# Retention and a gated feed-forward on one core: y's factors on GpSimd, four VectorE operations per weight tile, loads held by landings, a new order in the first third

## The chip and the metric

One core of a Trainium2 chip. The metric is the time of one execution on the device in microseconds (us). The engines are named as in the profile: PE is TensorE's matmul, PEld its weight load, DVE is VectorE, ACT is ScalarE, POOL is GpSimd, SP is SyncE, which here issues every DMA.

## What is computed

Inputs q, k, v have shape 4 x 8 x 768 x 64 (batch, head, time, width). In float32:

```python
for t in range(S):
    state = gamma[None, :, None, None] * state + np.einsum('bhd,bhe->bhde', k[:, :, t], v[:, :, t])
    y[:, :, t] = scale * np.einsum('bhd,bhde->bhe', q[:, :, t], state)
...
h = np.maximum(x @ w_in, 0.0)
...
for k in range(K):
    conv_out += conv_w[k][None, None, :] * hp[:, k:k + S, :]
gate = 1.0 / (1.0 + np.exp(-conv_out))
return (h * gate @ w_out).astype(np.float32)
```

gamma depends on the head alone, x is y with its heads side by side (4 x 768 x 512), hp is h with a row of zeros at both ends of time, K is 3, w_in is 512 x 1024 and w_out 1024 x 512. The weights arrive as 64-bit floats, and the kernel makes 32-bit floats of them itself, from their two 32-bit words.

## The kernel before

**Retention.** A chunk is 64 steps of time of two batches and eight heads; there are 24, twelve for each pair of batches. `scores` (L396 through `multiply`) multiplies k and q, `masked` (L423) multiplies the scores by a triangular mask, `scale_v` (L364 on ACT, L367 on DVE) scales v by powers of gamma, `mix` sends the masked scores times v and, from chunk 3 on, the next chunk's scores to PE in alternation, and `across` sends q times the carried state and the update of the state. `carry` (L430) copies the state out of PSUM, `decay` (L437) multiplies y by a factor for the chunk, `gy`. The factors of a pair's eleven later chunks are one first factor `gy_0`, loaded, times one number per chunk and head; `make_gy` (L354) makes them for four chunks at a time on DVE. `x_head` (L447, ACT) and `x_rest` (L453, DVE) split y into a coarse part and its rest, which PE takes in the format that the profile calls fp32r.

**Weights.** There are 16 tiles of 128 x 512, tiles 0 to 7 of w_in and 8 to 15 of w_out, and one 128 x 24 tile (number 16) of the convolution's weights. A tile is loaded (`load_w`, L463, 512 KB) and then made float32: `w_abs` on ACT (L481, absolute value of the high word), then on DVE `w_clamp` (L486), `w_shift` (L491), `w_sign` (L499), `w_power` (L507), `w_low` (L515, the low word times a power of two). `w_head` (L532, ACT) is the coarse part, `w_rest` (L547) the rest, and `w_add` (L562) adds the low word to the rest. Seven operations of a tile are on DVE.

**Feed-forward.** A unit is two chunks (twelve units). `mm1` (L576) multiplies a unit by one tile of w_in, 12 matmuls of 256 columns; from unit 6 on, units are taken in pairs by `prod` (L696) with sums of weight blocks made by `sum_w`, `w_head_t` and `w_rest_t`. `relu`, `conv_tap`, `conv_side`, `gate`, `gated`, `g_head`, `g_rest` follow on ACT and DVE, `seam` copies border columns on POOL (L744, L746), `mm2` (L793) multiplies by w_out, six matmuls of 512 columns a call, `put` and `store` write out.

**What sets the order.** Each engine takes its instructions in the order of the list `ORDER`, written out by hand; buffers are chosen by the strings in `SLOTS` and the addresses in `PLACES`. All loads and stores go through SP's queue in the order of the list, so one that waits holds the later ones. A load waits for its buffer; `HELD` adds a wait for a computing step to seven of them. Chunks 0 to 3 (`ALONE`) are loaded in two halves, `load` (q and k, L335) and `load_kv` (k and v, L339), 512 KB each; later chunks in one load of 1024 KB. There are three buffers `rw` for chunks. At the start PE runs `FILL` products of no use (L318), and `WARM` names a step ahead of which three shorter ones (L312) stand.

Of the kernel before, what the change touches and what calls it, by code (L numbers as in the profile page):

```python
# [59 lines left out]

WARM = {
    "mix/0": 3,
# [26 lines left out]
    scale_v/5 w_rest/4 w_clamp/16 w_low/4 relu/1/0 mm1/1/3 w_shift/16 load/7 scale_v/6 w_sign/16 w_add/4 w_power/16
    w_low/5 mix/5 relu/1/1 decay/4 w_abs/6 w_rest/5 across/5 w_clamp/6 w_low/16 w_add/5 mm1/1/4 carry/5 load/8  # L90
    decay/5 load_w/8 x_head/4 masked/6 w_abs/7 mm1/0/4 w_shift/6 w_add/16 w_sign/6 w_power/6 w_head/6 mix/6
    make_gy/2 conv_tap/0/2 across/6 w_clamp/7 scale_v/7 w_shift/7 masked/7 mm1/0/5 load/9 load_w/9 w_sign/7 carry/6
    conv_tap/0/3 w_low/6 mm1/1/5 relu/0/2 w_rest/6 w_head/7 seam/0/2/0 w_power/7 seam/0/1/0 w_add/6 mix/7 w_rest/7
    w_abs/8 across/7 w_low/7 x_head/5 relu/1/2 w_add/7 mm1/0/6 load/10 x_rest/4 w_clamp/8 x_rest/5 mm1/0/7 w_shift/8
    scale_v/9 w_sign/8 mm1/2/0 relu/0/3 masked/8 w_abs/9 scale_v/8 carry/7 mm1/2/1 w_power/8 w_head/8 load_w/10
    w_clamp/9 conv_tap/0/0 load_w/11 decay/7 mm1/1/6 w_shift/9 w_low/8 w_sign/9 mix/8 decay/6 w_head/9 scale_v/10
    across/8 masked/9 seam/0/0/0 seam/0/2/2 seam/1/2/0 mix/9 x_head/6 x_head/7 carry/8 w_power/9 relu/2/0
    conv_tap/0/1 conv_side/0/0/0 w_rest/8 w_add/8 load/11 seam/2/0/0 conv_tap/0/4 seam/5/0/2 seam/0/1/2 seam/0/0/2
    decay/8 masked/10 conv_side/0/4/0 w_low/9 seam/1/0/2 conv_side/0/1/0 x_rest/6 conv_side/0/1/2 mm1/1/7 relu/1/3
    mm1/2/2 mm1/2/3 mm1/2/4 mm1/2/5 w_abs/10 w_clamp/10 w_shift/10 w_abs/11 conv_side/0/0/2 gate/0/0 w_clamp/11  # L100
    gated/0/0 w_shift/11 across/9 carry/9 w_rest/9 w_sign/10 w_power/10 x_head/8 relu/2/1 x_rest/7 relu/2/2 x_rest/8
    mix/10 across/10 carry/10 decay/9 conv_side/0/3/2 w_sign/11 conv_side/0/2/0 x_head/9 mm1/3/2 mm1/3/3 relu/3/1
    mm1/3/4 mm1/3/5 g_head/0/0 w_add/9 w_power/11 w_low/11 conv_side/0/2/2 g_rest/0/0 mm2/0/1/0/0 masked/11 x_rest/9
    conv_tap/0/5 conv_side/0/5/2 conv_side/0/4/2 w_low/10 decay/10 conv_side/0/5/0 relu/3/2 seam/2/2/2 seam/1/0/0
    scale_v/11 load/12 w_head/11 w_rest/11 w_add/11 mm2/0/0/0/0 mix/11 masked/12 across/11 decay/11 load/13
    conv_tap/0/6 scale_v/12 w_head/10 conv_side/0/3/0 gate/0/1 w_rest/10 gated/0/1 across/12 load_w/14 w_abs/14
    w_clamp/14 mix/12 decay/12 masked/13 conv_tap/0/7 seam/2/2/0 seam/1/1/0 seam/4/2/0 carry/12 load_w/13 w_abs/13
    w_clamp/13 w_shift/13 mm1/2/6 mm1/2/7 relu/2/3 load/14 mm1/3/0 mm1/3/1 w_shift/14 w_sign/14 g_head/0/1 mm1/4/4
    mm1/4/5 w_add/10 g_rest/0/1 mm2/0/0/1/0 w_power/14 w_sign/13 w_head/13 mm2/0/1/1/0 seam/0/3/2 relu/3/0
    scale_v/13 mix/13 across/13 conv_side/0/7/2 seam/1/2/2 seam/1/3/0 seam/2/1/2 seam/2/1/0 w_power/13 w_low/13  # L110
    conv_tap/1/0 conv_side/1/0/2 w_head/14 seam/3/3/0 conv_side/0/6/2 conv_side/1/0/0 w_rest/13 scale_v/14 w_add/13
    seam/0/3/0 seam/3/1/0 conv_side/0/7/0 gate/0/2 x_head/10 gated/0/2 seam/4/0/0 seam/1/1/2 seam/2/0/2 seam/2/3/0
    conv_side/0/6/0 load_w/12 conv_tap/1/1 conv_side/1/1/0 conv_side/1/1/2 gate/0/3 x_head/11 gated/0/3 masked/14
    g_head/0/2 g_rest/0/2 gate/1/0 relu/4/2 w_abs/12 gated/1/0 w_clamp/12 x_rest/11 conv_tap/1/4 conv_tap/1/5
    conv_side/1/5/2 conv_side/1/4/2 load_w/15 w_abs/15 w_clamp/15 w_shift/12 w_shift/15 w_low/14 w_sign/15
    w_power/15 w_rest/14 mm1/3/6 mm1/3/7 relu/3/3 mm1/4/0 mm1/4/1 w_head/15 w_sign/12 carry/13 w_head/12 relu/4/0
    w_add/14 w_power/12 w_low/12 w_rest/12 conv_side/1/4/0 seam/1/3/2 mm1/4/2 mm1/4/3 relu/4/1 load/15 x_rest/10
    mix/14 across/14 mm1/4/6 mm1/4/7 g_head/1/0 carry/14 g_rest/1/0 mm1/5/2 mm1/5/3 w_low/15 conv_side/1/5/0
    conv_tap/1/6 gate/1/2 w_add/12 decay/14 diff/0/0/3 gated/1/2 seam/3/1/2 g_head/0/3 g_rest/0/3 conv_tap/1/2
    mm2/0/1/2/0 w_rest/15 w_add/15 conv_side/1/2/2 g_head/1/2 conv_tap/1/7 conv_side/1/6/0 masked/15 conv_tap/1/3  # L120
    scale_v/15 sum_w/0/7 conv_side/1/7/0 conv_side/1/6/2 relu/5/1 mm2/0/0/2/0 mm2/0/1/3/0 mm2/0/0/3/0
    conv_side/1/3/0 conv_side/1/7/2 conv_side/1/2/0 conv_side/1/3/2 gate/1/1 put/0/1/0 g_rest/1/2 gated/1/1
    g_head/1/1 load/16 mix/15 seam/6/3/0 seam/3/0/0 gate/1/3 across/15 carry/15 conv_tap/2/4 conv_tap/2/5 mm1/5/4
    mm1/5/5 seam/2/3/2 scale_v/16 diff/0/0/1 seam/3/2/0 mm2/1/0/0/0 g_rest/1/1 mm2/1/0/1/0 mm2/1/0/2/0 gated/1/3
    conv_side/2/4/2 sum_w/0/0 conv_tap/2/0 conv_side/2/0/2 g_head/1/3 g_rest/1/3 conv_tap/2/2 put/0/0/0 mm2/1/1/0/0
    mm2/1/1/1/0 diff/0/0/2 conv_side/2/5/2 sum_w/0/8 sum_w/0/9 conv_side/2/5/0 decay/15 conv_side/2/4/0 masked/16
    gate/2/2 conv_tap/2/1 head/0/0/0 decay/13 diff/0/1/3 conv_side/2/0/0 gated/2/2 g_head/2/2 diff/0/1/1
    conv_side/2/1/2 conv_side/2/1/0 conv_side/2/2/0 load/17 scale_v/17 g_rest/2/2 conv_tap/2/6 conv_tap/2/7
# [743 lines left out]
```

## Time and profile before

| what | us |
|---|---|
| median of 3 runs (lowest, highest) | 334.76 (332.27, 334.77) |
| span of the profiled execution | 331.0 |
| PE busy in it | 322.2 |
| DVE busy | 288.7 |
| ACT busy | 215.0 |
| POOL busy | 26.1 |

The page gives the profiled execution's span, from its first to its last instruction; its time as a run is not listed apart, and what lies around the span is read from the median of the runs. An engine counts as busy while it works on an instruction of its own; fill products count too. In the lists of the trace an engine's idle time stands in brackets before the instruction that ended it, with the engine or transfer that released it.

### The profile page before, as it was taken

The numbers are of one execution on the slowest core, as the hardware profiler recorded it, in microseconds if no ns is written. First come the engines' busy times: TensorE is split into PE (matmuls) and PEld (weight loads), VectorE is DVE, ScalarE is ACT, GpSimd is POOL, SyncE is SP. The second block draws the span as 40 slices with busy tenths as digits, with TensorE's granted clock in tenths as the row PEclk, the third lists the DMA queues.
The fourth block names the chain that finished last, engine by engine and source line by source line (L and its number), as shares of the span: only waits on it lengthen the run. The fifth ranks groups of instructions, "written<-read, shape, count | busy, mean of one in ns | idle before, by whom it ended". The sixth has DMA issues, their size and how long they took to land.

```text
span 331.0 us, 10761 instructions
## 1 busy us (share of the span) xinstructions
PE 322.2 (97%) x4642; PEld 289.4 (87%) x4642; DVE 288.7 (87%) x566; ACT 215.0 (65%) x448; POOL 26.1 (8%) x100
## 2 busy tenths in 40 slices
PE   8888999999999999899999999999999999999996
PEld 3778999999999988798888989999999888987885
DVE  3999999999999999897999998779988887869980
ACT  4657774756666475755939664965796866776761
...
GB/s 256 386 331 338 251 311 266 197 159 239 180 168 153 130 100 63 160 264 139 51 192 34 34 0 35 34 2 7 25 34 0 64 1 64 3 63 0 65 63 63
DMA packets 10415, 40.77 MB, mean 123 GB/s; under 512 B 1280, under 2 KB 1792, under 8 KB 7808
## 3 DMA queue, kind: packets, MB, share of 16 engines
...
q8 instruction: 36, 0.59, 0.7%
q14 instruction: 11, 0.09, 0.1%
...
## 4 chain that ended last, share of the span: by engine, by line
PE 94%; DMA 4%; issue 0%; ACT 0%; DVE 0%; ACTq 0%
PE ps_o L793 40%; PE ps_m L576 20%; PE ps_m L696 8%; PE ps_y L696 8%; PE ps_s L396 5%; PE ps_st L396 4%; DMA rw<-in_qkv 4%; PE ps_y L396 4%; PE ps_s L696 3%; PE ps_o L318 2%; PE ps_o L312 0%; ACT rw L364 0%; ACT o_sb L800 0%; DVE o_sb L304 0%; ACTq L800 0%
## 5 line engine op out<-in xcount | busy, mean ns | idle before, releaser
L576 PE MATMUL ps_m<-xu,wi_hi 128*128 128x256 f32 x384 | 68.8, 283 | 0.0
L793 PE MATMUL ps_o<-h,g 128*128 128x512 f32 (+1 forms) x200 | 62.7, 382 | 0.0
L576 PEld LDWEIGHTS ps_m<-xu,wi_hi 128*128 128x128 f32 x384 | 58.4, 189 | 0.9
L576 PE MATMUL ps_m<-xu,wi_lo 128*128 128x256 f32 x192 | 53.5, 279 | 0.0
L764 ACT ACTIVATE cv<-cv 128x512 f32<-128x512 f32 x48 | 29.8, 630 | 34.0 <-DVE cv L758 34.0
L396 PE MATMUL ps_y<-rw 64*64 64x64 f32 x1472 | 48.4, 220 | 0.1
L396 PEld LDWEIGHTS ps_y<-rw 64*64 64x64 f32 x1472 | 45.2, 135 | 0.7 <-ACT rw L629 0.4
L793 PEld LDWEIGHTS ps_o<-h,g 128*128 128x128 f32 x200 | 37.2, 188 | 7.1 <-ACT o_sb L800 0.4
L779 DVE TENSOR_TENSOR g<-cv,g 128x512 fp32r<-128x512 f32 x48 | 32.6, 687 | 8.1 <-ACT g L774 7.4
L758 DVE SCALAR_TENSOR_TENSOR cv<-h,cw_sb,cv 128x256 f32<-128x256 f32 x84 | 38.7, 478 | 1.0 <-ACT cv L753 0.4
L774 ACT CAST g<-cv 128x512 fp32r<-128x512 f32 x48 | 29.3, 617 | 11.7 <-DVE cv L769 10.3
L576 PEld LDWEIGHTS ps_m<-xu,wi_lo 128*128 128x128 f32 x192 | 36.1, 188 | 0.0
L396 PEld LDWEIGHTS ps_s<-rw 64*64 64x64 f32 x768 | 24.4, 135 | 8.6 <-issue 3.2
L396 PE MATMUL ps_s<-rw 64*64 64x64 f32 x768 | 27.6, 221 | 4.0 <-DMA rw<-in_qkv 1.5
L396 PE MATMUL ps_st<-rw 64*64 64x64 f32 x704 | 25.0, 219 | 0.5 <-ACT rw L364 0.5
L364 ACT ACTIVATE rw<-rw,consts_sb 128x128 f32<-128x128 f32 x64 | 20.4, 391 | 6.4 <-DMA rw<-in_qkv 6.4
L396 PEld LDWEIGHTS ps_st<-rw 64*64 64x64 f32 x704 | 22.6, 135 | 1.5 <-ACT rw L364 1.0
L753 ACT ACTIVATE cv<-h,cw_sb 128x256 f32<-128x256 f32 x42 | 20.5, 504 | 2.0 <-DVE g L779 2.0
L800 ACT COPY o_sb<-ps_o 128x512 f32<-128x512 f32 (+1 forms) x25 | 13.9, 561 | 11.8 <-PE ps_o L793 11.7
L423 DVE TENSOR_TENSOR rw<-ps_s,consts_sb 128x512 f32<-128x512 f32 x24 | 16.4, 684 | 5.2 <-PE ps_s L396 5.2
L793 PE MATMUL ps_o<-h_m,g 128*128 128x512 f32 (+1 forms) x50 | 19.1, 384 | 0.0
L793 PE MATMUL ps_o<-h_s,g 128*128 128x512 f32 (+1 forms) x50 | 19.1, 384 | 0.0
(256 smaller groups left out, 758.4 us busy)
## 6 DMA issues: line engine op xcount, KB each, us to landing
...
```

What stands on the lines that cost most here:

```text
L364: nc.scalar.activation(v[:, :, g], v[:, :, g], AF.Copy, scale=by[:, g : g + 1])
L396: nc.tensor.matmul(out, lhsT, rhs, start=start, stop=stop, skip_group_check=True)
L423: nc.vector.tensor_tensor(out=rw[n][:, 1], in0=s_ps[n], in1=mask_sb.unsqueeze(1).broadcast_to([P, 2, NPAIR, C]), op=ALU.mult)
L576: nc.tensor.matmul(h_ps[u, p][:, odd], w[:, k, fs], x[:, k].rearrange("p b t -> p (b t)"), start=(i == 0), stop=(i == len(products) - 1),)
L696: nc.tensor.matmul(ps[:, i], w[k][:, fs], x[:, k].rearrange("p b t -> p (b t)"), start=(i == m == 0 and q in (1, 5)), stop=(m == len(produ ...
L753: nc.scalar.activation(cvs[u, p][:, i], hs[u, p][:, i, :, 1 : P + 1], AF.Copy, scale=cw_sb[:, f, 1:2])
L758: nc.vector.scalar_tensor_tensor(out=cv, in0=h[:, :, k : k + P], scalar=cw_sb[:, f, k : k + 1], in1=cv, op0=ALU.mult, op1=ALU.add)
L764: nc.scalar.activation(cvs[u, p], cvs[u, p], AF.Sigmoid)
L774: nc.scalar.copy(gs[u, p][:, 0], cvs[u, p])
L779: nc.vector.tensor_tensor(out=lo, in0=cvs[u, p], in1=hi.bitcast(F32), op=ALU.subtract)
L793: nc.tensor.matmul(ps, g, w[f][:, cs], start=(f == 0 and i == 0), stop=(f == NF - 1 and i == 2))
L800: nc.scalar.copy(o[:, :n], o_ps[u, t, h][:, :n])
```

## The change

- `make_gy` makes one chunk's factor at a time, on POOL instead of DVE, into two buffers in turn; it stands 22 times in the list.
- A weight tile: `w_abs` scales the value down while taking it; `w_low3`, new and on ACT, turns the low word into the three bits that are still wanted; `w_clamp` has one comparison; `w_join`, new on DVE, shifts and puts the three bits in; `w_sign` puts the sign in; `w_rest` writes the rest in place. `w_shift`, `w_power`, `w_low` and `w_add` are gone.
- Each load waits until an earlier load has landed: the nearest one with at least eight units (`AHEAD`) issued after it, where a half chunk or a weight tile counts four units, a whole chunk eight, the constants three and `gy_0` one. `HELD` is gone.
- The buffers that the sums of weights take among the three `rw` are taken when the first of them is written.
- `FILL` is 5 instead of 6, the three warm products stand before mix/2 instead of mix/0, and the list has a new order up to about the products of unit 6.

```diff
-GY_AT_ONCE = 4
+AHEAD = 8
+SIZES = {"load_consts": 3, "load_gy": 1, "load_kv": 4, "load_w": 4, "load": 4}
...
-FILL = 6
+FILL = 5
...
-    load_w/0 load_w/1 load/0 load_consts load_kv/0 load_w/2 load/1 load_kv/1 load_gy load/2 w_abs/0 w_clamp/0
-    w_shift/0 w_sign/0 w_abs/1 w_power/0 w_head/0 w_clamp/1 w_rest/0 scores/0 w_low/0 masked/0 scale_v/0 w_add/0
-    w_shift/1 w_abs/2 mix/0 w_sign/1 w_clamp/2 w_shift/2 carry/0 load_kv/2 scores/1 w_power/1 load/3 w_head/1
-    load_w/3 masked/1 load_w/16 scale_v/1 w_low/1 w_sign/2 mix/1 decay/0 across/1 make_gy/0 carry/1 w_head/2
-    w_rest/1 load_kv/3 scores/2 load/4 decay/1 scale_v/2 masked/2 x_head/0 w_add/1 scores/3 x_head/1 w_power/2
-    w_abs/3 x_rest/0 mix/2 x_rest/1 load_w/4 w_clamp/3 across/2 scale_v/3 w_shift/3 masked/3 mm1/0/0 load/5 w_low/2
-    load_w/5 w_rest/2 mm1/0/1 w_sign/3 decay/2 w_head/3 w_add/2 carry/2 mix/3 w_abs/16 w_power/3 w_abs/4 w_rest/3
...
+    load_w/1 w_abs/1 w_low3/1 w_clamp/1 w_join/1 w_sign/1 load/0 load_consts load_kv/0 scale_v/0 scores/0 load_kv/1
+    load/1 masked/0 mix/0 scores/1 masked/1 scale_v/1 load_w/2 w_abs/2 carry/0 mix/1 across/1 w_low3/2 load_w/3
+    w_abs/3 w_clamp/2 load/2 load_kv/2 w_join/2 w_clamp/3 w_sign/2 w_low3/3 load_gy w_join/3 load_w/0 load/3
+    scores/2 masked/2 w_sign/3 w_head/2 carry/1 make_gy/1 scale_v/2 w_head/1 decay/0 mix/2 decay/1 across/2 scores/3
+    w_head/3 load_kv/3 x_head/0 w_low3/0 x_rest/0 w_rest/2 load_w/16 x_head/1 x_rest/1 make_gy/2 seam/0/0/0
+    make_gy/3 load/4 w_abs/0 carry/2 mm1/0/2 scale_v/3 decay/2 w_rest/3 mm1/0/3 w_clamp/0 w_join/0 x_head/2
+    w_low3/16 masked/3 mix/3 w_sign/0 w_head/0 w_rest/0 w_rest/1 w_abs/16 across/3 scale_v/4 decay/3 x_rest/2
+    load_w/6 load_w/4 mm1/0/0 relu/0/1 mm1/0/1 x_head/3 w_low3/4 load_w/5 make_gy/5 x_rest/3 w_abs/4 relu/0/0
...
     def make_gy(n):
+        gys[n] = const.tile([P, NPAIR, C], F32, name="gy_sb", bufs=2)
+        nc.gpsimd.tensor_tensor(
+            out=gys[n], in0=gy_0, in1=gf[:, n % NC].unsqueeze(2).broadcast_to([P, NPAIR, C]), op=ALU.mult
         )
...
-        nc.scalar.activation(m, high.bitcast(F32), AF.Abs)
+        nc.scalar.activation(m, high.bitcast(F32), AF.Abs, scale=EXP_DOWN)
+    def w_low3(i):
+        low = pieces[i][0].bitcast(U32)
+        nc.scalar.activation(low, low, AF.Copy, scale=LOW_BITS)
...
-        nc.vector.tensor_scalar(out=m, in0=m, scalar1=EXP_LOW, scalar2=EXP_HIGH, op0=ALU.max, op1=ALU.min)
+        nc.vector.tensor_scalar(out=m, in0=m, scalar1=EXP_HIGH, scalar2=None, op0=ALU.min)
+    def w_join(i):
+        low, _, m = pieces[i]
+        mi = m.bitcast(I32)
+        nc.vector.scalar_tensor_tensor(
+            out=mi, in0=mi, scalar=3, in1=low, op0=ALU.logical_shift_left, op1=ALU.bitwise_or
         )
...
+    def behind():
+        between = 0
+        for load, size in reversed(loads):
+            if between >= AHEAD:
+                return load
+            between += size
```

The order of the retention steps and products on PE up to chunk 23 is, in the part that the prediction speaks of, before: `mix/17 across/17 mix/18 across/18 mm1/5/6 mm1/5/0`; after: `mix/17 across/17 mm1/4/3 mm2/1/1/0/0 mm2/1/0/1/0 mm2/1/1/1/0 mix/18 across/18`. Both have `mix/11 across/11 across/12 mix/12` with nothing between.

## Rows read from the trace of the kernel before

**Rows 1.** The page: shares of the span, the instruction queue, the chain by engine.
```profile
PE 322.2 (97%) x4642; PEld 289.4 (87%) x4642; DVE 288.7 (87%) x566; ACT 215.0 (65%) x448; POOL 26.1 (8%) x100
...
q8 instruction: 36, 0.59, 0.7%
...
PE 94%; DMA 4%; issue 0%; ACT 0%; DVE 0%; ACTq 0%
```

**Rows 2.** Waits of PE: us in total, times, longest.
```profile
PE ps_s L396 <- issue: 1.3, 1, 1.3
```

**Rows 3.** Stretches: PE, PEld, DVE, ACT, POOL busy (instructions), clock, DMA share, GB/s.
```profile
0.00:30.00 30.00, 25.57 (x572) 20.05 (x573) 23.13 (x42) 17.43 (x40) 0.38 (x7) 1.00 0.93 329
10.00:15.00 5.00, 4.08 (x149) 3.31 (x150) 4.35 (x9) 3.86 (x10) 0.00 (x0) 1.00 1.07 400
30.00:130.00 100.00, 100.00 (x2039) 94.36 (x2037) 97.96 (x194) 62.04 (x132) 9.78 (x30) 1.00 0.55 193
130.00:200.00 70.00, 68.71 (x1257) 60.52 (x1256) 65.46 (x128) 47.34 (x101) 3.93 (x17) 1.00 0.30 104
200.00:331.00 131.00, 127.95 (x781) 114.51 (x779) 102.12 (x205) 88.16 (x176) 12.01 (x46) 1.00 0.09 33
```

**Rows 4.** The chain in order of time: start us, us, what.
```profile
1.05 6.92 PE ps_o L318 x12
9.05 1.49 PE ps_o L312 x6
11.73 5.07 DMA rw<-in_qkv
17.35 8.26 DMA rw<-in_qkv
27.95 3.02 PE ps_m L576 x24
138.93 1.29 issue
204.25 1.36 PE ps_o L793 x6
```

**Rows 5.** Timelines of PE, ACT, DVE at the start: start us, us, what [idle before].
```profile
12.08 1.15 PE L396 MATMUL ps_s<-rw 64*64 64x64 f32 x32 [0.44 <-DMA rw<-in_qkv]
18.74 1.09 PE L396 MATMUL ps_s<-rw 64*64 64x64 f32 x30 [1.29 <-DVE rw L423]
21.63 0.50 PE L576 MATMUL ps_m<-xu,wi_hi 128*128 128x256 f32 x2
25.75 0.33 PE L396 MATMUL ps_s<-rw 64*64 64x64 f32 x4 [1.03 <-DMA rw<-in_qkv]
...
16.82 1.28 ACT L364 ACTIVATE rw<-rw,consts_sb 128x128 f32<-128x128 f32 x4 [0.28 <-DMA rw<-in_qkv]
...
19.54 1.28 DVE L453 TENSOR_TENSOR xu<-x,xu 128x512 fp32r<-128x512 f32 x2
```

**Rows 6.** Groups by line of DVE and ACT: busy us, mean ns, idle before.
```profile
L515 DVE SCALAR_TENSOR_TENSOR g<-g 128x512 f32<-128x512 uint32 x16 | 11.0, 686 | 0.1
L507 DVE TENSOR_SCALAR g<-m 128x512 int32<-128x512 int32 x16 | 6.7, 423 | 0.1
L562 DVE TENSOR_TENSOR wi_lo<-m,g 128x512 fp32r<-128x512 f32 x8 | 5.5, 685 | 0.1
L354 DVE TENSOR_TENSOR gy_sb<-consts_sb 128x1024 f32<-128x1024 f32 (+1 forms) x3 | 3.4, 1128 | 0.0
...
L481 ACT ACTIVATE m<-g 128x512 f32<-128x512 f32 x16 | 10.8, 684 | 5.0 <-DMA g<-in_w_in 4.6 <-DVE wi_lo L562 0.4
```

**Rows 7.** Groups by line of POOL: busy us, mean ns, idle before.
```profile
L744 POOL COPY h<-h 128x4 f32<-128x4 f32 x16 | 6.0, 387 | 116.7 <-ACT h L588 58.7 <-ACT h L585 52.7 <-DVE cv L769 5.3
...
L744 POOL COPY h_o<-h 128x4 f32<-128x4 f32 x1 | 1.2, 1170 | 1.2 <-ACT h L585 1.2
```

**Rows 8.** All weight loads (L463), issue to landing.
```profile
DMA to landing us min/median/max: 3.3/5.8/8.5
```

More of the change, by code (lines that the diff above doesn't have):

```diff
@@ L89 @@
[L89 to L128, printed above, removed]
@@ new lines @@
+    w_clamp/4 make_gy/4 w_join/4 w_clamp/16 mm1/1/0 mm1/1/1 mm1/1/2 mm1/1/3 w_sign/4 w_head/4 masked/4 w_abs/5
+    w_low3/5 w_clamp/5 w_join/5 w_sign/5 w_rest/4 w_low3/6 w_abs/6 carry/3 load/5 w_clamp/6 w_head/5 w_rest/5
+    w_join/6 w_join/16 mix/4 across/4 load/6 load_w/7 masked/5 w_sign/16 relu/1/0 scale_v/5 mm1/0/4 mm1/0/5 w_low3/7
+    carry/4 relu/1/1 mix/5 across/5 load_w/8 load_w/10 w_sign/6 decay/4 w_head/6 load/7 w_rest/6 relu/0/2 w_low3/8
+    w_abs/7 x_head/4 mm1/1/6 mm1/1/4 w_clamp/7 w_join/7 decay/5 w_sign/7 w_abs/8 w_clamp/8 masked/6 w_low3/10
@@ new lines @@
+    scale_v/6 carry/5 mm1/1/5 x_head/5 scale_v/7 relu/1/2 mix/6 w_head/7 across/6 carry/6 w_rest/7 mm1/0/6 mm1/0/7
+    load/8 load_w/12 w_low3/12 w_abs/12 x_rest/5 masked/7 mix/7 across/7 x_rest/4 w_clamp/12 load_w/9 conv_tap/0/0
+    conv_tap/0/2 w_low3/9 w_abs/9 w_join/8 w_sign/8 w_head/8 relu/0/3 mm1/1/7 mm1/2/0 mm1/2/1 w_clamp/9 w_join/9
+    relu/1/3 conv_tap/0/1 carry/7 mm1/2/6 conv_side/0/0/0 make_gy/6 seam/0/1/0 decay/6 x_head/6 conv_tap/0/3
+    w_sign/9 w_head/9 load/9 scale_v/8 masked/8 w_rest/8 make_gy/9 make_gy/7 w_abs/10 w_clamp/10 decay/7 seam/0/0/2
@@ new lines @@
+    conv_tap/0/6 mix/8 w_join/10 scale_v/9 w_sign/10 w_rest/9 seam/2/0/0 seam/1/0/0 make_gy/8 seam/0/3/0 seam/0/1/2
+    relu/2/0 seam/1/0/2 across/8 mm1/2/7 mm1/2/2 carry/8 load_w/14 seam/0/2/2 seam/2/1/0 masked/9 decay/8 w_join/12
+    conv_side/0/1/0 conv_side/0/1/2 load_w/13 load/10 conv_side/0/2/2 conv_side/0/0/2 conv_tap/0/7 x_rest/6 relu/2/3
+    w_abs/14 gate/0/0 x_head/7 w_clamp/14 mix/9 across/9 carry/9 masked/10 scale_v/10 conv_side/0/3/0 gated/0/0
+    mm1/2/3 conv_side/0/3/2 mm1/2/4 w_sign/12 load/11 w_low3/14 w_join/14 w_sign/14 mix/10 across/10 g_head/0/0
@@ new lines @@
+    x_head/8 x_rest/8 x_rest/7 g_rest/0/0 w_head/10 mm1/2/5 w_rest/10 decay/9 masked/11 conv_side/0/6/0
+    conv_side/0/7/0 conv_side/0/2/0 relu/2/2 mm2/0/1/0/0 load/13 load_w/11 load/12 w_head/12 make_gy/11 seam/0/3/2
+    conv_side/0/7/2 conv_side/0/6/2 make_gy/10 seam/3/0/0 relu/2/1 seam/2/2/0 load_w/15 w_low3/11 mm1/3/2 w_low3/13
+    mm1/3/4 mm1/3/5 mm1/3/3 x_head/9 scale_v/11 carry/10 scale_v/12 w_head/14 w_abs/11 decay/10 x_rest/9
+    conv_tap/1/0 gate/0/1 mix/11 across/11 across/12 w_clamp/11 masked/12 w_join/11 gated/0/1 conv_tap/1/1 relu/3/2
@@ new lines @@
+    w_sign/11 w_rest/12 mix/12 sum_w/0/0 carry/12 gate/0/3 w_rest/14 decay/12 masked/13 relu/3/1 w_head/11 mm1/3/0
+    mm1/3/1 mm1/3/6 mm2/0/0/0/0 load/15 load/14 decay/11 conv_side/1/0/2 conv_side/1/1/0 w_rest/11 gated/0/3
+    w_abs/13 mm1/3/7 w_low3/15 conv_side/1/0/0 g_head/0/1 g_rest/0/1 g_head/0/3 relu/3/0 scale_v/15 scale_v/13
+    w_clamp/13 conv_side/1/1/2 sum_w/0/1 conv_tap/1/2 seam/1/3/2 seam/5/0/2 x_head/12 w_abs/15 mm1/4/4 w_join/13
+    scale_v/14 g_rest/0/3 w_sign/13 make_gy/13 seam/1/3/0 seam/4/0/0 seam/2/1/2 mix/13 seam/3/2/0 across/13
@@ new lines @@
+    seam/1/1/0 make_gy/16 conv_side/1/2/0 decay/13 masked/14 x_head/10 conv_tap/0/4 conv_tap/0/5 conv_tap/1/3
+    w_head/13 x_head/11 carry/13 conv_side/0/4/2 sum_w/0/2 relu/3/3 gate/1/0 w_rest/13 seam/1/2/2 conv_side/0/5/2
+    gated/1/0 make_gy/15 seam/1/1/2 conv_side/1/2/2 mm1/4/5 mm2/0/1/1/0 seam/0/2/0 conv_side/0/4/0 relu/4/2
+    conv_side/0/5/0 w_clamp/15 mix/14 gate/0/2 across/14 load/16 seam/1/2/0 mm1/4/0 mm1/4/6 conv_side/1/3/2
+    conv_side/1/3/0 gate/1/1 carry/14 masked/15 w_join/15 gated/0/2 w_sign/15 g_head/0/2 g_rest/0/2 mix/15
@@ new lines @@
+    g_head/1/0 across/15 w_head/15 mm2/0/0/1/0 mm2/0/0/2/0 gated/1/1 masked/16 decay/15 x_rest/10 w_rest/15
+    mm2/0/1/2/0 mm2/0/0/3/0 mm1/4/7 g_rest/1/0 conv_tap/1/4 g_head/1/1 carry/15 scale_v/16 g_rest/1/1 x_head/13
+    sum_w/1/0 conv_tap/2/0 conv_tap/1/5 conv_side/1/4/2 conv_tap/2/1 conv_side/2/1/0 relu/4/3 conv_tap/1/6
+    seam/2/0/2 seam/5/2/0 seam/5/3/2 make_gy/14 conv_side/2/0/2 conv_side/1/5/2 decay/14 conv_tap/1/7 put/0/0/0
+    diff/0/0/3 x_rest/13 conv_side/1/4/0 load/18 scale_v/18 conv_side/2/0/0 conv_side/1/7/0 conv_side/1/5/0 load/17
```

271 lines of the change are left out of this document (116 added, 155 removed).

## The prediction

> **What bounds the kernel now.** I read the shares first, then the waits of PE, then PE by stretches, then the chain in order of time, and only for the first 30 us PE's own instructions. The shares [rows 1] put PE at 322.2 of 331.0 us and the chain at 94% PE: TensorE sets the time, and whatever another engine saves is worth only what it takes off PE's idle time. The stretches [rows 3] say where that is. From 30 to 130 us PE is busy for 100.00 of 100.00 us, although DVE has 97.96 us of work beside it; from 200 us on the only idle time is the last copy and store, and the order of steps there does not change. What is left is 30.00 - 25.57 = 4.4 us before 30 us and 1.3 us between 130 and 200. But fill work counts as busy, so the first stretch has more to give than its idle time: the real question is when the products of the chunks and mm1 come.
>
> The chain [rows 4] shows the start as two transfers, 11.73 to 16.80 and 17.35 to 25.61, and then PE alone. PE's own rows [rows 5] say the same: it waits for data at 12.08 and 25.75, for VectorE at 18.74, begins mm1 (L576) at 21.63, and loses 1.03 us again at 25.75 for chunk 4, whose scores are mixed into chunk 3. My yardstick is one point that both kernels have in common: chunks 0 to 3 done (mix and across) and four blocks of mm1. Before, that is 27.95 + 3.02 = 30.97 us [rows 4]; after it PE never starves but once. The once is at 138.93: 1.29 us of "issue" [rows 2, 4], in which no engine is waited for. It falls where the old order sets mix/17, across/17, mix/18, across/18 with no other product between: 512 small weight loads and matmuls at one go. I take it for a wait for PE's own code, since a DMA queue of kind "instruction" stands in the page [rows 1]; no row ties that queue to the gap.
>
> **Part by part.**
>
> VectorE's weights. Each of 16 tiles loses w_shift and w_power (0.42 each), w_low (0.686) and w_add (0.685), and gains w_join, which is a two-operand operation with a strided operand like w_low (0.686) [rows 6]. That is 2.22 - 0.69 = 1.53 us, times 16: 24.5 us. w_clamp drops one of two comparisons in one instruction; I leave it at 0.42, as w_power's row (bounds: half of that, and 0.43). The 24-wide conv tile is a few times 0.2. make_gy takes 3.4 us off as well. DVE should fall from 288.7 to about 261 us. After 30 us this is worth nothing at once, since PE is full there with the old load; it is slack. Before 30 us it pays, and is in the sum below.
>
> w_low3 on ScalarE. Nearest row: w_abs, the same shape and the same stride, 0.684 [rows 6]. It also writes with a stride; bounds 0.6 and, if the second stride cost as much again as the whole, 1.37; taken 0.68, or 0.6 from start to start where operations follow each other. 16 of them are 11 us on an engine that is busy 62.04 of 100.00 us [rows 3]: hidden, except for the first two or three.
>
> make_gy on GpSimd. No row shows a GpSimd product. From below: VectorE made all eleven in 3.4 us, 0.31 each [rows 6]. From above: 1.17, the longest GpSimd copy [rows 7]. I take 0.31 plus 0.39, which GpSimd needs on average to copy four elements: 0.7. 22 of them bring GpSimd from 26 to some 41 us. It has ample time; the question is only whether a decay waits, below.
>
> Here the Trainium skill speaks against the change. Rows first: a copy of four elements per partition takes from 0.39 on average up to 1.17 us on GpSimd [rows 7], so something holds it up. The Trainium skill, "SBUF — State Buffer", section "Who interferes with whom", says that a VectorE instruction with two SBUF inputs and a GpSimd instruction that reads SBUF exclude each other for the whole of an instruction. The uneven copies agree with that rule. By it up to 22 times 0.7 = 15 us of VectorE's 28 saved would go back; by the rows alone nothing does.
>
> Loads that wait for landings. A load now waits until the nearest earlier load with 8 units (1 MB, by the table of sizes) issued behind it has landed: about three half-MB loads are under way. Queued behind a waiting load on SP are all later loads, and the stores, which are far later. The DMA engines are full from 10 to 15 us at 400 GB/s [rows 3]; a half-MB load is then 1.31 us, and three are 3.93 us. From issue to landing the weight tiles took 3.3 us at the least and 5.8 at the median [rows 8], the latter with more queued ahead. So the hold costs nothing if a load that finds little ahead of it lands within 3.9 us. I take nothing, with 3.3 nearest to such a load; the other end is a rival.
>
> New order at the start. The loads go w1, chunk 0, constants, w2, w3, ... and each step can be dated. Scores/1 began at 12.08 on its landing [rows 5], when 3.23 MB had been asked for ahead of and with it (six half-MB loads and 80 KB); with 0.40 MB per us, any load lands at 12.1 + (MB - 3.23)/0.40. In the new order: q, k of chunk 1 2.70 MB, 10.8 us; w2 12.1; w3 13.4; q, k of chunk 2 14.7; k, v of chunk 2 16.0; y's first factor 16.3; w0 17.6; chunk 3 18.9 and 20.3; chunk 4 (7.57 MB) 22.9.
> PE: the fill is one of six shorter (the six take 6.92 us [rows 4], the last ones less than the first), scores/0 follow at about 7, mix/0 about 9.3, scores/1 at 10.8, masked/1, mix/1 and across/1 until 14.7, scores/2 until 15.9, the warm-up until 17.4 (1.49 us before [rows 4]; it lies in a wait, and would cost that if the wait were gone).
> VectorE up to there has clamp, join and sign of w2 and w3, join/3, masked/2 (16.5), sign/3 (17.1), decay/0 (17.7), decay/1 (18.3), each 0.6 from start to start (two took 1.28 us from 19.54 [rows 5]). The factor for decay/1 can start at 16.3 and is due at 17.7, so even 1.17 us is covered.
> ScalarE runs head/2, carry/1, then the four scalings of chunk 2's v, 1.28 us as at 16.82 [rows 5]: 16.4 to 17.7. mix/2 and across/2 end at 19.5, scores/3 at 20.6. ScalarE goes on with head/1, head/3, x_head/0, w_low3/0, x_head/1, five times 0.5 to 0.6: 20.4. x_rest/1 on VectorE ends at 21.0. mm1 begins at 21.1, half a us before 21.63: ScalarE's queue is late next, not the data.
> Then two blocks of mm1 (3.02 us [rows 4]) to 24.1; chunk 4 landed at 22.9, so the old wait at 25.75 is gone; masked/3 is ready at 23.8 (decay/2, rest/3, clamp/0, join/0, masked/3 after 21.0). mix/3 and across/3 take 2.2 us (25.75 to 27.95 before [rows 4, 5]): 26.3. The other two blocks need w_rest/0 (25.7) and w_rest/1 (26.3, only the second): 29.3. The yardstick moves from 30.97 to 29.3: **1.7 us gained.**
>
> The rest of the order. The new order has at least two blocks of mm1, mm2 or prod (1.36 us for one of mm2 [rows 4], more for the others) between any two chunks from chunk 4 to 23, but for 11 and 12, which stand together in the old order too without a wait there: the waits of PE list one such gap only [rows 2]. So the 1.3 us at 138.93 go. Chunks 4 on are 1 MB a load and have three buffers until chunk 23, since the weight sums take theirs only when written; no starving there.
>
> **Sum.** 331.0 - 1.7 - 1.3 = 328.0 us of span. The page gives no time beside the span; the median of the three runs is 334.76, 3.76 above it, and I carry that along: 331.8 us. A change of 1% (3.35 us) is about what can be told from none.
>
> **The rivals.**
> - *More at the start.* ScalarE need not be late: its operations run 0.5 apart, and in the sum they stand behind low-priority weights. If mm1 begins as soon as scores/3 are through with chunk 3's landing (18.9 + 1.1 = 20.0), 1.1 us more: 330.7. For it: VectorE has 1.53 us less to do per tile; against it: the queues are in order, and head/1 and low3/0 do stand ahead.
> - *The factors hold VectorE.* Three factors (1, 2, 3) fall before the yardstick. If VectorE stands still for each, 3 times 0.7 = 2.1 us, the whole 1.7 us is lost and only the 1.3 us stay: 333.5. The uneven copies [rows 7] speak for it, the cover of decay/1 against. The rule of the Trainium skill above, "Who interferes with whom", would give this.
> - *The holds drain the DMA queue* (slower). If a load takes the median 5.8 us [rows 8] to land even with only two others under way, a half MB costs 5.9/3 = 1.96 us instead of 1.31. Chunk 4 ends 13.4 such steps behind the first landing: 8.7 us later, 31.6 instead of 22.9, and mix/3, which had 1.2 us to spare, starts 7.5 us later: 339. It decides at 3.9 us from issue to landing. For it: the median; against it: the median was taken with three or more loads ahead, and the shortest is 3.3.
> - *It does less than it says:* PE is full from 30 us, so 28 us less on VectorE give nothing; that is in my sum already, and is why it is so small.
>
> **How the numbers follow.** Forecast 0.50 at 331.8; the line of 1% is at 331.4, and with an error of about 1 us in the start I put 0.22 of the 0.50 under it. More at the start 0.19, faster. The factors 0.16, within 1%. The drained queue 0.15, slower. So faster 0.22 + 0.19 = 0.41, the same 0.28 + 0.16 = 0.44, slower 0.15. The range goes from 329.5 (the first rival and 1 us) to 335.5 (a landing of 4.7 us, which costs 3.5 us at chunk 4); the full drain and some tails are left out. The likeliest case alone is 330.5 to 333.
>
> **What would show it.** DVE near 261 us, ScalarE near 226, GpSimd near 41; the first L576 near 21.1 and the fourth block done near 29.3; no "issue" gap of over 1 us in PE's waits; the DMA engines still full until 28 us. It is wrong if PE waits for x tiles, weights or decays after 30 us, if the DMA share falls before 25 us (the drain), or if VectorE idles while GpSimd works.

## The result, and the profile after

| kernel | median us (runs) | lowest to highest | span of the profiled execution |
|---|---|---|---|
| before | 334.45 (4) | 332.27 to 334.77 | 331.0 |
| after | 338.04 (4) | 337.47 to 340.00 | 335.7 |

The change makes the kernel slower by a little over 1%, clear of the noise: ratio 1.0145, with an interval of 1.0098 to 1.0193. The forecast was 331.8 us, the range ended at 335.5. In all runs the time is 1.8 us above the span (after: 337.47 for a span of 335.7), not the 3.76 that the forecast carried along; the profiled execution of before was one of its quick ones.

The page of after, shares and the chain by engine, against [rows 1]:

```profile
PE 325.3 (97%) x4640; PEld 291.1 (87%) x4640; DVE 271.6 (81%) x512; ACT 223.7 (67%) x465; POOL 46.1 (14%) x122
...
PE 45%; DVE 27%; DMA 12%; ACT 9%; issue 4%; POOL 1%; SPq 0%; ACTq 0%; DVEq 0%
```

VectorE lost 17 us, as was meant, and PE's share is the same 97%. But the chain was 94% PE and is 45% PE now: over half of the time another engine or a transfer decides when PE goes on. PE's share doesn't show it: PE's busy time itself grew by 3.1 us, with two fill matmuls fewer. The profile models where matmuls end, so short stalls may lie inside that time; this is a reading that no run here tests. Nor does the chain say how much time is lost, as the kernels below will show.

The waits of PE after, against [rows 2]:

```profile
PE ps_st L395 <- ACT rw L429: 1.7, 1, 1.7
PE ps_s L395 <- DMA rw<-in_qkv: 1.6, 3, 0.9
...
PE ps_y L395 <- DVE x L435: 0.7, 1, 0.7
```

The "issue" gap of 1.3 us is gone, and a wait of 1.7 us for `carry` has come. Stretches of after, columns as in [rows 3]:

```profile
0.00:30.00 30.00, 24.37 (x555) 18.65 (x556) 16.68 (x27) 18.45 (x43) 3.49 (x9) 1.00 0.87 299
10.00:15.00 5.00, 2.94 (x147) 2.69 (x142) 1.61 (x3) 3.25 (x9) 0.00 (x0) 1.00 0.90 331
10.00:25.00 15.00, 11.83 (x355) 10.60 (x350) 10.60 (x17) 11.42 (x27) 3.29 (x5) 1.00 0.91 323
30.00:130.00 100.00, 98.72 (x2246) 92.71 (x2245) 86.91 (x159) 70.70 (x149) 21.14 (x38) 1.00 0.63 222
```

The transfers of the start ran at 331 GB/s where [rows 3] have 400, and PE is no longer full from 30 to 130 us. PE's timeline at the start of after, against [rows 5]:

```profile
13.95 0.27 PE L395 MATMUL ps_st<-rw 64*64 64x64 f32 x2 [1.72 <-ACT rw L429]
...
23.47 0.51 PE L534 MATMUL ps_m<-xu,wi_hi 128*128 128x256 f32 x2
...
27.43 0.33 PE L395 MATMUL ps_s<-rw 64*64 64x64 f32 x4 [0.94 <-DMA rw<-in_qkv]
...
29.56 0.50 PE L534 MATMUL ps_m<-xu,wi_hi 128*128 128x256 f32 x2
...
32.30 0.28 PE L534 MATMUL ps_m<-xu,wi_lo 128*128 128x256 f32 x1
```

mm1 begins at 23.47 instead of 21.63, chunk 4 is waited for until 27.43 instead of 25.75, and the third and fourth block of mm1 begin at 29.56. Their last matmul gives the yardstick: 32.30 + 0.28 = 32.6 us, 1.6 later than before and 3.3 later than forecast. How far one profile can be trusted in this, the last experiment shows: b_split, whose start is that of before, has the same point at 32.2 us and not at 30.97. The other 3.1 us of the span come after the yardstick, net of the 1.3 us of the gap. The chain in order of time shows what PE waited for there (after, 36 to 84 us; start us, us, what):

```profile
36.01 4.34 DMA g<-in_w_in
...
40.42 6.78 DMA rw<-in_qkv
...
47.26 6.67 DMA g<-in_w_out
...
59.91 1.02 DVE rw L366
...
76.67 0.61 DVE g L742
77.32 1.19 PE ps_o L756 x4
```

Three transfers in a row, each issued as the one before it landed, hold the chain until 54 us; then ScalarE and VectorE, which got their weights late, hold it until 77. Before, the chain is PE from 28 us on but for that gap [rows 1, 4].

### The profile page after: what moved, and what is told of

Same layout as the page of the kernel before. It is cut to its first block, busy times and chain, and to the rows that moved or that the text cites. A ratio compares the mean times of both kernels' runs of the same rounds, so it can differ in the third digit from the quotient of the medians.

```text
span 335.7 us, 10755 instructions
## 1 busy us (share of the span) xinstructions
PE 325.3 (97%) x4640; PEld 291.1 (87%) x4640; DVE 271.6 (81%) x512; ACT 223.7 (67%) x465; POOL 46.1 (14%) x122
## 4 chain that ended last, share of the span: by engine, by line
PE 45%; DVE 27%; DMA 12%; ACT 9%; issue 4%; POOL 1%; SPq 0%; ACTq 0%; DVEq 0%
PE ps_o L756 27%; DMA rw<-in_qkv 8%; DVE cv L721 8%; PE ps_m L534 5%; PE ps_y L659 5%; PE ps_m L659 4%; DMA g<-in_w_in 3%; DVE g L742 3%; DVE m L583 2%; DVE cv L732 2%; DMA g<-in_w_out 2%; DVE rw L422 2%; ACT cv L716 2%; DVE x L435 2%; PE ps_s L395 2%
## 5 line engine op out<-in xcount | busy, mean ns | idle before, releaser
L534 PE MATMUL ps_m<-xu,wi_hi 128*128 128x256 f32 x384 | 69.6, 283 | 0.0
L756 PE MATMUL ps_o<-h,g 128*128 128x512 f32 (+1 forms) x175 | 53.6, 384 | 0.1
L395 PE MATMUL ps_y<-rw 64*64 64x64 f32 x1472 | 49.1, 220 | 1.3 <-DVE x L435 0.7
L721 DVE SCALAR_TENSOR_TENSOR cv<-h,cw_sb,cv 128x256 f32<-128x256 f32 x100 | 46.0, 486 | 4.4 <-ACT cv L716 1.8
L756 PEld LDWEIGHTS ps_o<-h,g 128*128 128x128 f32 x175 | 32.4, 188 | 6.9 <-DVE g L742 0.5
L742 DVE TENSOR_TENSOR g<-cv,g 128x512 fp32r<-128x512 f32 x48 | 33.4, 704 | 6.0 <-ACT g L737 5.3
L354 POOL TENSOR_TENSOR gy_sb<-consts_sb 128x256 f32<-128x256 f32 x22 | 18.3, 833 | 98.2 <-DVE x L435 67.7
L716 ACT ACTIVATE cv<-h,cw_sb 128x256 f32<-128x256 f32 x50 | 23.7, 502 | 1.5 <-DVE g L742 1.4
L732 DVE TENSOR_TENSOR cv<-h,cv 128x512 f32<-128x512 f32 x25 | 17.2, 687 | 5.1 <-ACT cv L727 4.9
```

Of the source, the lines that this page charges most:

```text
L395: nc.tensor.matmul(out, lhsT, rhs, start=start, stop=stop, skip_group_check=True)
L534: nc.tensor.matmul(h_ps[u, p][:, odd], w[:, k, fs], x[:, k].rearrange("p b t -> p (b t)"), start=(i == 0), stop=(i == len(products) - 1),)
L716: nc.scalar.activation(cvs[u, p][:, i], hs[u, p][:, i, :, 1 : P + 1], AF.Copy, scale=cw_sb[:, f, 1:2])
L721: nc.vector.scalar_tensor_tensor(out=cv, in0=h[:, :, k : k + P], scalar=cw_sb[:, f, k : k + 1], in1=cv, op0=ALU.mult, op1=ALU.add)
L732: nc.vector.tensor_tensor(out=cv, in0=hs[u, p][:, :, :, 1 : P + 1], in1=cv, op=ALU.mult)
L742: nc.vector.tensor_tensor(out=lo, in0=cvs[u, p], in1=hi.bitcast(F32), op=ALU.subtract)
```

## The experiments

Theory: the loads that wait for landings keep too little under way, so that data come late. Rivals: GpSimd's factors hold VectorE; the new order loses time by its own waits. Runs that stood side by side on one chip are compared by their times, others by their ratio to the kernel before, which ran at 333.55 to 334.49 us beside them.

**Holds: none, longer, longest.** The kernel after with one number changed:

```diff
-AHEAD = 8
+AHEAD = 10**6
```

a_nohold, no load waits for a landing:

> The changed kernel with the waits for landings taken out, and nothing else. Theory drain (the waits leave the DMA engines short of work: 8.86 MB had come by 30 us against 9.68 MB before, and chunk 4 landed at 27.3 us): about 9.6 MB by 30 us, chunk 4 lands before 25 us, the first mm1 begins before 22 us, and the time falls by 3 to 5 us to 333 to 335 us. Theory factors (GpSimd's factors hold VectorE up) and theory order (the new order puts VectorE's and ScalarE's work where PE has to wait): still 337 to 339 us.

Measured: 336.38 us, ratio 1.0067 (1.0042 to 1.0093). Then AHEAD = 12 and AHEAD = 16.

a_ahead12:

> The kernel after with AHEAD 12 instead of 8 (1.5 MB issued behind the load that is waited for). Theory 'the holds starve the DMA engines': half of what AHEAD 16 gives, 337. Rival 'the loss lies in the order': 338.

a_ahead16:

> The kernel after with AHEAD 16 instead of 8: a load waits for a landing with 2 MB issued behind it instead of 1 MB, so about five half-MB loads are under way instead of three. Theory 'the holds of 1 MB starve the DMA engines': the throughput from 10 to 25 us rises from 316 to 331 GB/s towards the 400 of a_nohold, chunk 4 lands 2 us earlier than at 27.3, and the time is 336 or a little less, between a_nohold and after or under both, since code still gets through. Rival 'the loss lies in the order, not in the data': 338 as after.

Measured: AHEAD 12 337.06 us, ratio 1.0106 (1.0064 to 1.0148); AHEAD 16 335.62 us, 1.0070 (1.0044 to 1.0097), and on another chip 335.52, 1.0032 (1.0009 to 1.0056; a_ahead16_again, below). So 1.0145, 1.0106, 1.007, 1.0067 for 8, 12, 16 and none: the holds of 1 MB cost 0.75% to 1.1%, by the two runs with AHEAD 16, which is 2.5 to 3.8 us; those of 2 MB can't be told from none. The rows of the second run with AHEAD 16, stretches and chain:

```profile
10.00:15.00 5.00, 3.16 (x136) 2.77 (x126) 2.47 (x5) 3.52 (x8) 0.00 (x0) 1.00 1.02 407
...
30.00:130.00 100.00, 99.65 (x2252) 94.02 (x2251) 87.64 (x161) 70.53 (x150) 21.11 (x38) 1.00 0.60 213
```

```profile
40.19 3.02 PE ps_m L534 x24
...
45.24 4.43 PE ps_m L534 x36
...
56.74 5.85 PE ps_m L534 x48
```

The transfers are back at 407 GB/s, and the chain from 30 to 78 us is PE alone in this run; no transfer and no VectorE stands in it. But mm1 does not begin earlier:

```profile
15.45 0.56 PE L395 MATMUL ps_y<-rw 64*64 64x64 f32 x12 [0.64 <-issue]
...
21.90 0.62 PE L395 MATMUL ps_y<-rw 64*64 64x64 f32 x14 [1.00 <-issue]
23.39 0.50 PE L534 MATMUL ps_m<-xu,wi_hi 128*128 128x256 f32 x2
```

23.39 against 23.47: ahead of it PE now waits twice in "issue", 1.64 us in all. Over the profiles of the new order PE's waits for transfers sum to 1.6 to 2.1 us in the three with AHEAD 8 and to 0.6 or less in the nine with more or none; the waits in "issue" follow no such order (0.9 to 4.2 us in the three, 2.1 to 3.5 in the nine). The yardstick, as the end of the 48th matmul of mm1, lies at 32.4 to 33.7 us in the four with AHEAD 8 or 12 and at 31.6 to 33.6 in the other eight, but from there to the end the four need 303.1 to 303.9 us and the eight 299.9 to 302.1. So it is behind the start that the holds cost most of their time.

**Landing holds in the old order.** b_hold is the kernel before with the `behind` wait instead of `HELD`, b_wgh has every part of the change but the order (and, with it, `FILL`, `WARM` and the buffers of the sums).

```diff
-HELD = {...}
+AHEAD = 8
```

b_hold:

> The kernel before with the waits for landings of the changed one in place of its own seven waits for computing steps, and nothing else. Theory drain: slower than before by 2 to 5 us (336 to 339 us), with less than 9.3 MB by 30 us. Theories factors and order: within 1 us of before.

b_wgh:

> The kernel before with every part of the change but the order: four VectorE operations a weight tile, one factor a chunk on GpSimd, loads held by landings instead of HELD; the old order (and FILL, WARM and the sum buffers as before). Theory 'the new order is made for the landing holds, and the loss lies in the holds': 340 or more, as the 342.5 of b_hold, with issue gaps of several us in PE's waits; the order would then be worth 2 to 4 us of gain. Rival 'the new order itself loses time': at or under 336, below the kernel after.

Measured: b_hold 342.51, ratio 1.0264 (1.0229 to 1.03); b_wgh 342.38, 1.021 (1.0152 to 1.0267). The holds cost the old order 7 to 9 us, with the light VectorE as without it. PE's waits in b_hold:

```profile
PE ps_st L395 <- issue: 4.7, 3, 2.1
PE ps_s L395 <- issue: 1.6, 2, 1.5
PE ps_y L395 <- issue: 1.5, 1, 1.5
```

Most of it is "issue", where waits for data had been expected. It is not all: the granted clock fell too, to 0.66 from 45 to 50 us in b_hold, and to 0.74 and 0.58 from 20 to 25 and 25 to 30 in b_wgh. The new order loses less: with the same parts it runs at 338.04 (1.0145 against 1.021), so under these holds it is worth 2 to 4 us.

**What "issue" is.** b_w is the kernel before with the new weight operations alone. w_low/4, which held load/7, doesn't exist there, and w_join/4 held it; b_w2 is the same with a later step.

```diff
-    "load/7": "w_join/4"
+    "load/7": "w_join/16"
```

b_w:

> The kernel before with weights by four VectorE operations a tile (and the new one on ScalarE), in the old order. Every theory: VectorE falls by 24 us to about 264 us. If PE alone sets the time, within 1 us of before; if VectorE's load costs PE its small waits (20.7 us of waits and fill in the whole span before), 1 to 3 us faster.

b_w2:

> The kernel before with the new weight operations (w_low3, w_join), as in b_w, but load/7 held by w_join/16 instead of w_join/4, so that it is issued near 36.5 us instead of 34.2. Theory 'code queues behind loads': in b_w PE's one 2.9 us gap at 40 came since load/7 went ahead of PE's code; with the later hold the gap is gone and the span is 334.7 - 2.9 = 331.8, or lower by what the lighter VectorE gives (down to 330), time 333 to 334. Rival 'the new weight operations cost PE time by themselves': the gap or another of its size stays, 336.

Measured: b_w 336.01, ratio 1.0068 (1.0049 to 1.0087); b_w2 333.99, 1.0009 (0.9973 to 1.0044). SP's timeline in b_w (start us, us from the first issue to the end of the second) and PE's longest wait:

```profile
34.17 10.25 SPq L330 DMA_DIRECT2D rw<-in_qkv  x2
```

```profile
PE ps_st L391 <- issue: 2.9, 1, 2.9
```

and SP's in b_w2:

```profile
37.37 4.44 SPq L330 DMA_DIRECT2D rw<-in_qkv  x2
```

One 1 MB load issued at 34.17 instead of 37.37 makes a PE gap of 2.9 us at 40, in which no engine and no data are waited for; issued later, the gap is gone. In the trace's records of the instruction queue the fetch that PE needs there starts at 40.5 in b_w, 37.7 in before. The other records agree. In the 20 traces PE has 58 gaps of "issue" of over 0.15 us, and every one ends 1.2 to 1.6 us after a 16 KB transfer of that queue: in b_w the transfer ends at 41.56 and PE goes on at 43.04, in before it ends at 138.84 and PE goes on at 140.22. This is the row that the prediction lacked for its gap at 138.93. So "issue" at PE is a wait for its code, and in b_w the code comes behind the data that were asked for ahead of it. The hold of load/7 in `HELD` lets code through; the other six were not tried in this way. Fewer bytes under way do not let it through by themselves: b_hold, with holds of 1 MB, waits longest in "issue". What counts seems to be which load goes out just ahead of the code. b_w2 answers another question too: 20 us less on VectorE (268.6 of 288.7) give nothing.

**Factors.** a_gyold is the kernel after with the old `make_gy`, four chunks at a time on VectorE; b_wg is b_w2 with the new one, and b_wg2 the same with load_kv/3 held by carry/1 instead of decay/0.

```diff
-        nc.gpsimd.tensor_tensor(out=gys[n], in0=gy_0, ...)
+        nc.vector.tensor_tensor(out=gy_sb[:, cs], ...)
```

a_gyold:

> The changed kernel with the factors made as before, for four chunks at a time on VectorE (3.4 us in all), at the places of the first factor of each four. Theory factors: VectorE's busy time falls from 271.6 to about 264 us, the spells of 1.1 us in weight operations near 18 to 21 us are gone, and the time falls by 2 to 4 us to 334 to 336 us. Theory drain and theory order: within 1 us of 338 us.

b_wg:

> The kernel before, old order and HELD, with four VectorE operations a weight tile (as b_w2) and one factor a chunk on GpSimd; no landing holds. Theory 'factors on GpSimd cost PE nothing': 334, as b_w2, and then the 342.4 of b_wgh against it is the price of the landing holds in the old order. Rival 'factors hold VectorE': a decay or an x_rest of the start comes late, 335.5 or more, and DVE's busy time rises from 268.6 towards 275.

b_wg2:

> As b_wg (old order and HELD, four VectorE operations a weight tile, one factor a chunk on GpSimd), but load_kv/3 is held by carry/1, which ends near 16.6 us, instead of decay/0, which ended at 16.0, so that it is issued at the same time as in b_w2 (16.75). Theory 'the 0.5% of b_wg came from that load, which went ahead of chunk 4': ratio 1.001 as b_w2. Rival 'factors on GpSimd cost the old order half a per cent themselves': 1.006 as b_wg.

Measured: a_gyold 339.18, ratio 1.0154 (1.0120 to 1.0188), no gain; b_wg 336.33, 1.0057 (1.0008 to 1.0105); b_wg2 335.74, 1.0032 (0.9994 to 1.0069). The last two lie above b_w2, but the intervals overlap, and both profiles show a lowered clock at the start that b_w2's doesn't (last section). Under the holds of 1 MB the factors can't be seen, so the old `make_gy` went into the kernel with AHEAD 16:

a_ahead16_gyold:

> The kernel after with AHEAD 16 and the factors made for four chunks at a time on VectorE again, as before. With AHEAD 16 alone the ratio was 1.007. Theory 'what is left beside the holds is the new order (more changes between small and large products, a code gap, a late chain on VectorE)': the ratio stays at 1.007, 335.6. Rival 'what is left is GpSimd's factors, which hold VectorE': the ratio falls to 1.002 or less, 334.3, and DVE's busy time falls from 271.6 to about 268.6.

Measured: 334.69, ratio 1.0006 (0.9980 to 1.0033), against 1.007 on another chip. So both ran again side by side.

a_ahead16_again:

> The kernel after with AHEAD 16, as a_ahead16, on one chip beside the two other kernels of this call, since the runs of before differ by up to 0.8 us between chips. Theory 'GpSimd's factors cost what is left': 0.9 us or more above a_ahead16_gyold_again. Rival 'the order costs it, and the difference between the two earlier ratios (1.007 and 1.0006) was that of the chips': within 0.4 us of it.

a_ahead16_gyold_again:

> The kernel after with AHEAD 16 and the factors on VectorE. Theory 'GpSimd's factors cost what is left': ratio 1.000 to 1.003, 0.9 us or more under a_ahead16_again. Rival 'the order': 1.005 to 1.007, the same as a_ahead16_again.

Measured: 335.52, ratio 1.0032 (1.0009 to 1.0056), with the factors on GpSimd; 334.69, 1.0008 (0.9979 to 1.0037), on VectorE. The difference of 0.83 us falls between what the two theories had expected, next to the first. It has the same sign in the first pair, on two chips, and in a third (335.28 against 334.88, with carry/0 moved, both below); as a size, some 0.4 to 0.9 us, it is an estimate, since the intervals overlap. The chain by engine differs more clearly, here in a_gyold, a_ahead16_again and a_ahead16_gyold_again:

```profile
PE 85%; DMA 8%; DVE 4%; issue 1%; ACT 1%; SPq 0%; ACTq 0%
...
PE 66%; DVE 19%; ACT 6%; DMA 3%; issue 3%; POOL 1%; ACTq 0%; DVEq 0%
...
PE 89%; DVE 4%; DMA 3%; ACT 1%; issue 1%; ACTq 0%
```

In the new order PE has 45 to 69% of it in the eight profiles with the factors on GpSimd and 85 to 97% in the four with them on VectorE, so the 45% of after are in part theirs. But this is no measure of lost time: a_gyold is as slow as after. Nor do the two costs add: with the factors on VectorE the holds of 1 MB cost 1.5% (1.0154 against 1.0006 and 1.0008), about 5 us.

What GpSimd does to VectorE is plain in three of the groups, busy us and mean ns, of a_ahead16_again and then of a_ahead16_gyold_again:

```profile
L742 DVE TENSOR_TENSOR g<-cv,g 128x512 fp32r<-128x512 f32 x48 | 33.9, 713 | 6.0 <-ACT g L737 5.3
L496 DVE SCALAR_TENSOR_TENSOR m<-g,m 128x512 int32<-128x512 int32 x16 | 11.2, 703 | 0.1
L451 DVE TENSOR_TENSOR xu<-x,xu 128x512 fp32r<-128x512 f32 x14 | 10.2, 734 | 0.2
```

```profile
L745 DVE TENSOR_TENSOR g<-cv,g 128x512 fp32r<-128x512 f32 x48 | 32.6, 686 | 6.1 <-ACT g L740 5.3
L499 DVE SCALAR_TENSOR_TENSOR m<-g,m 128x512 int32<-128x512 int32 x16 | 11.0, 685 | 0.1
L454 DVE TENSOR_TENSOR xu<-x,xu 128x512 fp32r<-128x512 f32 x14 | 9.5, 684 | 0.1
```

On the mean of all of them, these operations take 27, 18 and 50 ns more each where GpSimd makes the factors; other groups are unchanged (the 25 `TENSOR_TENSOR` of cv 688 against 686). The pages give DVE 271.6 us with the factors on GpSimd and 268.0 with them on VectorE: moving 3.4 us of work [rows 6] off VectorE made it busy 3.6 us longer.

**carry/0.** The 1.7 us wait at 13.95 comes from ScalarE's queue:

```profile
12.76 0.66 ACT L471 ACTIVATE m<-g 128x512 f32<-128x512 f32 x1 [1.75 <-DMA g<-in_w_in]
13.32 0.57 ACT L429 COPY rw<-ps_st 128x512 f32<-128x512 f32 x1
```

carry/0 stands behind w_abs/2, which waits for its weights until 12.76. Three kernels have carry/0 ahead of it: with AHEAD 8, without holds, with AHEAD 16.

```diff
-load_w/2 w_abs/2 carry/0 mix/1
+carry/0 load_w/2 w_abs/2 mix/1
```

a_carry:

> The kernel after with carry/0 moved ahead of load_w/2 and w_abs/2 in the list, nothing else. Theory 'the start loses 1.7 us to carry/0 behind w_abs/2': PE's wait of 1.7 us for the state's copy at 13.95 is gone, the first mm1 comes up to 1.5 us earlier, and 338.0 falls to 336.5. Rival 'the next landing bounds the start (load/2 at 16.3, chunk 4 at 27.3)': the wait only moves to scores/2 and chunk 4, and the time stays within 0.5 us of 338.

a_nohold_carry:

> The kernel after with both edits of earlier runs: no load waits for a landing (as in a_nohold), and carry/0 ahead of load_w/2 and w_abs/2 (as in a_carry). Theory 'without the holds the data are early enough, and then the order of carry/0 bounds the start': PE's wait for the state's copy (1.2 us in a_nohold) goes, and the time falls by about 1 us below a_nohold, to 335.4. Rival 'carry/0 is hidden behind the next thing in any case': 336.4 as a_nohold, with the idle time moved to a wait for VectorE, ScalarE or code before the first mm1.

a_ahead16_carry:

> The kernel after with AHEAD 16 and carry/0 ahead of load_w/2 and w_abs/2. Theory 'with more data under way the order of carry/0 bounds the first 15 us': PE's wait of 1.2 us for the state's copy goes and the ratio falls from 1.007 to 1.003 or 1.004. Rival 'another wait of the start takes its place': 1.007.

Measured: 338.07, ratio 1.0119 (1.0081 to 1.0156); 335.49, 1.0060 (1.0032 to 1.0088); 335.28, 1.0036 (1.0012 to 1.0060). None can be told from the kernel without the edit. PE's timeline of a_ahead16_carry shows why:

```profile
16.44 0.39 PE L392 MATMUL ps_y<-rw 64*64 64x64 f32 x6 [2.18 <-issue]
```

The wait for the copy is gone, and PE runs into its missing code at once.

**All three off.** AHEAD 16, factors on VectorE, carry/0 first. a_ahead16_carry_gyold:

> The kernel after with the three edits that helped: AHEAD 16, factors on VectorE, carry/0 ahead of w_abs/2. If the three are independent (0.75%, 0.5% and 0.3%), the ratio is 0.998, a little faster than before; if carry/0 only uncovers another wait, it is 1.001, as a_ahead16_gyold; if the order holds the rest, 1.004.

Measured: 334.88, ratio 1.0005 (0.9982 to 1.0028). The order without its burdens is as fast as the old one, not faster. No version beats the kernel before.

**The gap at 138.93.** b_split is the kernel before with two calls of mm2 between chunks 17 and 18.

```diff
-mm2/1/1/3/0 mm2/1/0/3/0 mix/17 across/17 mix/18
+mix/17 across/17 mm2/1/1/3/0 mm2/1/0/3/0 mix/18
```

b_split:

> The kernel before with two calls of mm2 (mm2/1/1/3/0, mm2/1/0/3/0) moved from ahead of mix/17 to between across/17 and mix/18, nothing else. If the 1.3 us of issue at 138.93 is PE outrunning its code in 512 small products in a row, the gap is gone and the time falls by 1.3 us, to 333.1. If the gap is a wait of another kind, or the time is made up elsewhere, it stays at 334.4.

Measured: 334.10, ratio 0.9995 (0.9958 to 1.0033). The issue wait shrinks from 1.3 [rows 2] to 0.7 us:

```profile
PE ps_s L393 <- issue: 0.7, 1, 0.7
```

Half a us is below what these runs resolve; the time decides nothing here. The same kernel shows how much one profile varies: its first 100 us are the old ones, yet its longest wait for VectorE there is 2.7 us where [rows 5] have 1.29.

## Why the prediction was wrong

The account, in times of different chips: before 334.1, the new order with AHEAD 16 and old factors 334.7 (not told from before), factors on GpSimd 335.5 (+0.8), AHEAD 8 338.0 (+2.5). The forecast was a gain of 3.0 us in the span (1.7 and 1.3), the account is a loss of 3.9: of the 6.9 us between them, 3.6 are the gain that did not come, 2.5 the holds and 0.8 the factors.

- **The first step that failed is the price of the holds**: "I take nothing, with 3.3 nearest to such a load", with 3.9 us as the point from which it decides. Issue to landing in after, of the weight loads and then of all `load` steps (min, median, max us):

```profile
DMA to landing us min/median/max: 3.2/4.3/7.5
...
DMA to landing us min/median/max: 4.3/5.4/7.5
```

3.3 was right for the least and wrong for the typical load: of the chunk loads not one came under 3.9. Most of these are whole chunks; of half a MB each, the page of after has the half chunks at a median of 5.4 us, the tiles of w_in at 4.6 and those of w_out at 4.5. At 323 GB/s, the mean from 10 to 25 us, a half MB takes 1.62 us and three 4.9. The rival of the drained queue had the right mechanism and a chance of 0.15. With 1.62 for its 1.96 its working puts chunk 4 at 22.9 + 13.4 x 0.31 = 27.1 us, and PE had it at 27.43. But its 339, 1 us above the measured time, is near by luck: it laid the whole loss on chunk 4, where PE waits only 0.94 us, and with AHEAD 16 the yardstick is hardly earlier (31.6 and 32.5 us in its two profiles). What the holds cost came by a way that the prediction had excluded: "no starving there" after chunk 4, where in after loads of 1 MB and the weights wait for each other to 54 us. The range, too, ended at a landing of 4.7 us, which by the working of that rival is 2.3 us at chunk 4 and not 3.5, since 1.2 us were to spare.
- **The second step that failed is the gain of 1.7 us in the start.** The dates of the landings took the holds as free; with AHEAD 16, where they nearly are, mm1 still begins at 23.39 instead of 21.1, with the two waits for code ahead of it. The sum had no term for code in the start, although the prediction read 138.93 as such a wait. That code is what kept the gain away is read from the trace; no run takes these waits out. And 30.97, from which it was to be gained, is the number of one profile; b_split has 32.2 with the same start.
- **carry/0 was overlooked** (1.72 us at 13.95, by w_abs/2 ahead of it): the sum dated the scores and mixes by data, not by ScalarE's queue. Taken away it gives nothing, so it didn't decide.
- **The gap at 138.93 went, as forecast**, and its cause was read rightly. But such gaps come elsewhere: after has 0.38 us at 54.75 and 0.47 at 125.84, and a_ahead16_gyold 1.42 at 124.00. So the 1.3 us are not seen in the time.
- **VectorE's slack is worth nothing at once: right**, by b_w2. Its size was wrong: 271.6 instead of 261 us. The weight operations gave 20.1 (288.7 to 268.6 in b_w2), not 24.5: the sum took durations, but operations that follow each other overlap and start 0.6 us apart where one lasts 0.69, as the step on the start itself had it. And the factors stretch the rest.
- **The factors: own time nearly right** (0.83 us on average, 0.7 forecast), **effect on the sum mis-sized**: taken at nothing, they cost about 0.8 us. The rows above, 713 against 686 ns, say that VectorE is held. This is the rule of the Trainium skill, "SBUF — State Buffer", section "Who interferes with whom", that the prediction had weighed, and the trace agrees with it; VectorE's busy time grew by the 3.6 us above and the 3.4 that left it, 7.0 us for 18.4 us of products in a_ahead16_again, so a bit over a third of a product's time is lost to VectorE and not all of it.
- **The 3.76 us** between span and time were 1.8. By luck that error ran against the others: the span was missed by 7.7 us (335.7 for 328.0), the time by 6.2.

What stays open: by which waits the holds cost their time behind the start, since after shows transfers and VectorE on the chain from 36 to 77 us, and a_gyold, as slow, PE alone with two waits in "issue" of 0.90 and 1.52 us; and how the 0.6 us between the new order at its best and the kernel before divide, if they are any.
